# First batch on fp32 key chunks, values in column halves, a bound for A's scale

## The chip, the cores and the metric

The kernel runs on one core of one Trainium2 chip. The metric is the device time of one execution in microseconds (us), the median of several runs; a profile of one further execution shows where the time goes. Engines are named as in the profile: PE (TensorE), PEld (its weight loads), DVE (VectorE), ACT (ScalarE), POOL (GpSimd), SP (SyncE, which here only issues DMAs).

## The reference

Agent attention over 4 batches of 11456 tokens with 128 channels and 49 agents, then a mixture of 8 experts (128 to 1024 to 128) of which each token takes one:

```python
def _attn_ref(q, k, v, agents):
    a2k = sm(agents, k)          # softmax(scale * agents @ k^T): 49 x 11456 a batch
    agent_v = a2k @ v            # 49 x 128
    q2a = sm(q, agents)          # 11456 x 49
    return q2a @ agent_v
def _moe_ref(x, w_gate, w1, w2):
    expert_idx = np.argmax(x @ w_gate, axis=1)
    ...
    h = np.maximum(xe @ w1[e], 0.0)
    out[mask] = gate_w[mask, None] * (h @ w2[e])
```

## The kernel before

The 11456 tokens of a batch are 12 chunks: 11 of 128x8 tokens and a rest of 96x2. Per batch the kernel computes the key scores of all chunks and their maximum over the tokens, then exp and the sum of exp times values, which gives `av` (49 agents by 128 channels, twice side by side). From `av` it chooses the expert that most tokens are likely to take, loads that expert's w1 and w2 and forms A = av @ w1, so that for a query chunk the hidden layer is relu(E @ A), with E the exponentials of the query's scores, turned over by DMA (tile `M`). The loop over hidden layers, `experts`, has 184 steps a batch: `layer1` (L1204, L1205) multiplies 512 tokens by one 128-column piece of A in two fp16 parts `Ah`, `Al`; ACT and DVE make the two fp16 parts of its relu (`hh`, L1210, L1211); `layer2` (L1224) multiplies by w2. Tokens of other experts are left to gathered blocks at the end.

fp32 factors are split into two fp16 parts with a power-of-two scale. `prepare` does this for a chunk: `squares` (L332, ACT) gives the sum of squares, `scale_bits` (L212 to L219) the scale, then one of two forms. In form 'A', `split` (L360 on ACT, L362 on DVE) makes the parts `hl`, and `turn_over` (L387) transposes them by a DMA on SP's queue into `hT`. In form 'C' (keys of the first batch), `transposed` transposes the fp32 chunk on PE (L403), and ACT and DVE make the two parts from PSUM (L405, L406). `scores` then does three fp16 matmuls for each 128 tokens (L415 to L417). Values of the first batch are in form 'F': `values` multiplies fp32 exponentials by fp32 values (L522), whose output is 49 rows, and adds each chunk's result to `acc` (L533).

The first batch has nothing to run beside it: no hidden layer can start before its av, weights and A exist. Later batches do their attention in the shadow of the hidden layers of the batch before. Work is put on a list of events with due times in steps (`at`, `prepare`, the constants KS0 and so on), and the recording layer may then issue an instruction of an engine earlier if it is ready sooner. Chunks, w1 and w2 come into 11 buffers named `ld` (512 KB each) in turn; `load` asks for them `AHEAD` uses ahead. A load waits on SP's queue until the buffer of 11 tiles before is free. `weights` computes two column halves of A (`pa`, L734), their maximum (L741) and w2's (L743), a common scale (`pow2_scale`, over PE and DVE twice), and then Ah, Al (L755, L756) and w2's parts (L762, L763).

Of the kernel before, what the change touches and what calls it, by code (L numbers as in the profile page):

```python
# [22 lines left out]
A = 49  # L23
# [8 lines left out]
MODES = {'k': 'C', 'v': 'F', 'q': 'A'}  # L32
# [13 lines left out]
KS0, KT0, KL0, VT0, VL0, QS0, QT0, QL0 = -200, 2, 4, 2, 1, -146, 3, 5  # L46
# [20 lines left out]
AHEAD = 3  # L67
# [3 lines left out]
def agent_moe_kernel(ctx, tc, q, k, v, agents, wg, w1, w2, out):  # L71
# [33 lines left out]
    make_identity(nc, ident)  # L105
    ones = cpool.tile([P, P], F32, name="ones")
# [74 lines left out]
    def pow2_scale(amax, n):  # L181
# [9 lines left out]
        nc.tensor.matmul(pb[:, :n], ones[:n, :], dg[:n, :n], start=True, stop=True)  # L191
        pw = two.tile([P, 2], F32, tag="ppw", name="ppw")
# [11 lines left out]
    state = [dict() for _ in range(B)]  # L204

# [33 lines left out]
    def expert_weights(x, new, by_act=False):  # L239
# [6 lines left out]
        dma.dma_start(w2e, w2[ds(e, 1)].rearrange("e (p t) d -> (e p) (t d)", t=FT))  # L246
# [23 lines left out]
    def attention(b):  # L270
# [9 lines left out]
        def load(src, c):  # L280
            i = uses.index((b, src, c))
            for o in uses[:i + AHEAD]:
# [11 lines left out]
        def agent_squares():  # L294
            ag = AG["ag"] = one.tile([P, D], F32, tag="ag", name="ag")
            nc.sync.dma_start(ag[:A], agents[b])
# [14 lines left out]
        def agent_split():  # L311
            pt = small_ps()
            nc.tensor.transpose(pt[:, :A], AG["ag"][:A, :], ident[:A, :A])
            agh = AG["h"] = two.tile([P, A], F16, tag="agh", name="agh")
# [6 lines left out]
        def uniform(src, c):  # L321
            return src == "v" or how[src, c] == "C"

        def squares(src, c):
# [3 lines left out]
            x = load(src, c)  # L328
            jk = one.tile([P, CH], F16, tag="jk", name="jk")
# [6 lines left out]
        def total(src, c):  # L336
            p, ss = chunks[c][1], SC[src, c]
# [3 lines left out]
        def total2(src, c):  # L341
            if not uniform(src, c):
# [8 lines left out]
        def split(src, c):  # L351
            _, p, t = chunks[c]
# [41 lines left out]
        def transposed(src, c):  # L394
            _, p, t = chunks[c]
            x = load(src, c)
            xT = xpool.tile([P, 2, 8, P], F16, tag="hl", name="xT", bufs=HLB)
            m = SC[src, c][0][:, :1]
            for h in range(0, t, 4):
# [4 lines left out]
                pv = pt[:, :n * p].rearrange("d (i p) -> d i p", p=p)  # L404
                nc.scalar.activation(xT[:, 0, h:h + n, :p], pv, AF.Copy, scale=m)  # L405
# [17 lines left out]
        def kscores(c):  # L423
# [5 lines left out]
            pv, m = ps[:p, :t * A].rearrange("p (t a) -> p t a", a=A), SC["k", c][1][:p, :1]  # L429
            if first and c % 4 < SEV:  # L430
# [11 lines left out]
        def kmax(c):  # L442
# [7 lines left out]
            else:  # L450
                mx = MX["x"]
                nc.vector.tensor_tensor(mx[:p, :t, :], mx[:p, :t, :], sv, op=ALU.max)
# [32 lines left out]
        def kexp3(c):  # L485
            _, p, t = chunks[c]
            sc = S[c][:p, :t, :]
            if c == 0:
# [6 lines left out]
            if how["v", c] == "F":  # L495
                return
# [8 lines left out]

        def values(c):
            _, p, t = chunks[c]
            ps = either(first, psS, "s", psY, "y")
            if how["v", c] == "F":
                x, sc = load("v", c), S[c]  # L510
            else:
                (vh, vl), eh = TT.pop(("v", c)), EH.pop(c)
            for i in range(t):

                if how["v", c] == "F":
                    pairs = [(sc[:p, i, :], x[:p, i, :])]
                else:
# [855 lines left out]
```

## Time and profile before

| | us |
|---|---|
| median of 3 runs (1165.85 to 1166.94) | 1166.04 |
| the profiled execution: its own time | 1163.97 |
| its span, first to last instruction | 1162.2 |
| PE busy in the span | 1028.1 (88%) |
| DVE busy | 1016.7 (87%) |
| ACT busy | 840.4 (72%) |

The span is 1.8 us shorter than that execution's time, and that time is 2.07 us under the median. PE's granted clock is 0.961 of full speed over the span. Busy shares are averages: most of the span is the loop of hidden layers with PE and DVE both near 90%; the first 100 us, in which only the first batch's attention can run, look otherwise and are read stage by stage.

### The profile page before, as it was taken

How to read it: one execution, taken by the hardware profiler on the slowest of the kernel's cores; microseconds unless marked ns; L12 is line 12 of the kernel's file. 1: busy time of each engine (PE TensorE's matmuls, PEld its weight loads, DVE VectorE, ACT ScalarE, POOL GpSimd, SP SyncE). 2: the span in 40 equal slices, each digit the busy share in tenths (PEclk: the TensorE clock that was granted, in tenths of full speed). 3: DMA queues.
4: the chain of work that ended last, by engine and by line, in shares of the span. 5: the costliest groups of instructions: out<-in, count | busy, mean ns of one | idle time of the engine just before them, and what ended most of it. 6: DMA issues, size and time to landing. Idle time of an engine off the chain costs nothing. (4 is left out here: it accounts for less than half of the span.)

```text
span 1162.2 us, 36038 instructions
## 1 busy us (share of the span) xinstructions
PE 1028.1 (88%) x14607; PEld 827.9 (71%) x14607; DVE 1016.7 (87%) x2407; ACT 840.4 (72%) x1506; POOL 231.5 (20%) x369
## 2 busy tenths in 40 slices
PE   6757789988989989989988889999989988989895
PEld 5645668767867777777776677777767776767795
DVE  7867798889989988998989997999899988899794
ACT  8548786689669787798678885896585555756591
POOL 1301010035400110143300110245100213110133
PEclk9877999999998999999999999999999999999998
DMA  8489999371489899371499898450574544523370
GB/s 331 131 235 215 250 237 203 99 187 59 84 233 268 189 248 223 108 189 47 84 274 267 195 249 184 122 126 32 161 182 104 127 102 102 158 67 112 118 258 14
DMA packets 265673, 191.02 MB, mean 164 GB/s; under 512 B 217513, under 2 KB 230306, under 8 KB 265504
## 3 DMA queue, kind: packets, MB, share of 16 engines
q1 hardware_dynamic: 263648, 185.39, 62.9%
q0 software_dynamic: 1568, 2.25, 1.0%
q8 instruction: 115, 1.88, 0.7%
q10 hardware_dynamic: 288, 1.05, 0.3%
q14 instruction: 54, 0.44, 0.1%
HBM read 99.75 MB, written 36.43 MB: 117 GB/s over the span
## 5 line engine op out<-in xcount | busy, mean ns | idle before, releaser
L1224 PEld LDWEIGHTS <-hh 128*128 128x128 f16 x8640 | 555.4, 100 | 168.9 <-issue 9.8
L1224 PE MATMUL py<-w2h,hh 128*128 128x128 f16 (+1 forms) x5760 | 615.5, 222 | 4.2 <-issue 2.6
L1210 ACT ACTIVATE hh<-ph 128x512 f16<-128x512 f32 (+1 forms) x728 | 411.8, 586 | 183.0 <-PE ph L1205 164.4
L1224 PE MATMUL py<-w2l,hh 128*128 128x128 f16 (+1 forms) x2880 | 531.2, 222 | 0.0
L1211 DVE SCALAR_TENSOR_TENSOR hh<-ph,hh 128x512 f16<-128x512 f32 (+1 forms) x736 | 479.0, 667 | 47.1 <-ACT hh L1210 44.1
L1204 PE MATMUL ph<-M,Ah 128*128 128x512 f16 (+1 forms) x736 | 278.3, 378 | 26.1 <-DVE hh L1211 23.6
L1205 PE MATMUL ph<-M,Al 128*128 128x512 f16 (+1 forms) x736 | 279.0, 380 | 0.1
L362 DVE SCALAR_TENSOR_TENSOR hl<-ld,mul,hl 128x1024 f16<-128x1024 f32 (+1 forms) x120 | 147.7, 1234 | 13.6 <-ACT hl L360 13.1
L332 ACT ACTIVATE jk<-ld 128x1024 f16<-128x1024 f32 (+1 forms) x132 | 133.9, 1014 | 29.9 <-PE pa L734 10.4
L360 ACT ACTIVATE hl<-ld,mul 128x1024 f16<-128x1024 f32 (+1 forms) x120 | 130.7, 1095 | 21.2 <-DVE mul L216 20.4
L219 POOL TENSOR_SCALAR div<-hb,bits 128x1 int32<-128x1 int32 (+1 forms) x96 | 39.9, 425 | 363.5 <-DVE hb L212 312.8
L1205 PEld LDWEIGHTS <-Al 128*128 128x128 f16 x736 | 72.4, 98 | 33.5 <-issue 30.4
L1204 PEld LDWEIGHTS <-Ah 128*128 128x128 f16 x736 | 73.7, 100 | 6.3 <-issue 3.5
L415 PEld LDWEIGHTS <-hT 128*128 128x128 f16 (+1 forms) x630 | 53.2, 98 | 20.3 <-DMA hT<-hl 19.5
L415 PE MATMUL ps_s<-agh,hT 128*128 128x49 f16 x572 | 54.1, 187 | 14.8 <-DMA hT<-hl 11.0
L1237 DVE TENSOR_TENSOR yo<-py,cs 128x512 f32<-128x512 f32 (+1 forms) x92 | 61.3, 666 | 0.2 <-PE py L1224 0.2
L219 POOL TENSOR_SCALAR div<-hb 128x1 int32<-128x1 int32 (+3 forms) x45 | 14.0, 312 | 223.4 <-DVE hb L212 198.0
L416 PE MATMUL ps_s<-agl,hT 128*128 128x49 f16 x572 | 53.8, 186 | 0.0
L417 PE MATMUL ps_s<-agh,hT 128*128 128x49 f16 x572 | 53.7, 186 | 0.0
L416 PEld LDWEIGHTS <-hT 128*128 128x128 f16 (+1 forms) x630 | 52.1, 98 | 2.3 <-issue 1.7
L417 PEld LDWEIGHTS <-hT 128*128 128x128 f16 (+1 forms) x630 | 51.6, 98 | 0.3
L493 POOL TENSOR_TENSOR es<-es,S 128x392 f32<-128x392 f32 (+1 forms) x39 | 41.3, 1060 | 40.3 <-ACT S L483 31.7
(304 smaller groups left out, 1385.9 us busy)
## 6 DMA issues: line engine op xcount, KB each, us to landing
ld<-in_k_dram SPq DMA_DIRECT2D x44, 512.0 KB
ld<-in_v_dram SPq DMA_DIRECT2D x44, 512.0 KB
ld<-in_q_dram SPq DMA_DIRECT2D x44, 512.0 KB
out_dram<-yo SPq DMA_DIRECT2D x88, 256.0 KB
w1e<-in_moe_w_dram SPq DMA_DIRECT2D x17, 512.0 KB
w2e<-in_moe_w_dram SPq DMA_DIRECT2D x17, 512.0 KB
exps<-E SPq DMA_DIRECT2D x44, 196.0 KB
wn<-in_moe_w_dram SPq DMA_DIRECT2D x16, 512.0 KB
```

The costliest lines, as they stand in the source:

```text
L332: nc.scalar.activation(jk[:p, :t * D], x[:p, :t, :].rearrange("p t d -> p (t d)"), AF.Square, accum_out=ss[:p])
L360: nc.scalar.activation(hi[:p, :t, :], x[:p, :t, :], AF.Copy, scale=m)
L362: nc.vector.scalar_tensor_tensor(lo[:p, :t, :], x[:p, :t, :], m, hi[:p, :t, :], op0=ALU.mult, op1=ALU.subtract)
L415: nc.tensor.matmul(o, x[:, 0, i, :p], AG["h"], start=True, stop=False)
L416: nc.tensor.matmul(o, x[:, 0, i, :p], AG["l"], start=False, stop=False)
L417: nc.tensor.matmul(o, x[:, 1, i, :p], AG["h"], start=False, stop=True)
L1204: nc.tensor.matmul(ph[:, :nn], st['Ah'][:, f, :], m, start=True, stop=False)
L1205: nc.tensor.matmul(ph[:, :nn], st['Al'][:, f, :], m, start=False, stop=True)
L1210: nc.scalar.activation(hh[:, 0, :nn], ph[:, :nn], AF.Relu)
L1211: nc.vector.scalar_tensor_tensor(hh[:, 1, :nn], ph[:, :nn], 0.0, hh[:, 0, :nn], op0=ALU.max, op1=ALU.subtract)
L1224: mm_ = lambda l, r, **k: nc.tensor.matmul(o, l, r, skip_group_check=True, **k)
L1237: nc.vector.tensor_tensor(yo[:p, :n, :], py[:p, :n * D].rearrange("p (i d) -> p i d", d=D), cs.unsqueeze(2).broadcast_to([p, n, D]), op=AL ...
```

## The change

It rebuilds the first batch. Of its 12 key chunks four full ones and the rest are in a new form 'X', and its first query chunk too: no squares, no scale and no parts; the fp32 chunk is transposed on PE, copied from PSUM in two halves (one by ACT, one by DVE) and multiplied in fp32 (one matmul, no longer three) by the fp32 agents. The values' matmuls go in turn to two halves of PE's columns (output rows 0 to 48 and 64 to 112 of two PSUM tiles) and accumulate over all chunks; `both` adds the halves when the result is transposed. Of the subtractions of the maximum three go to POOL, and the sum of exponentials is kept in two accumulators, one on POOL, one on DVE. For all batches A's scale comes from a bound, max|w1| of a row times max|av|, summed over rows, and w2's from ACT's sum of squares, so neither needs A. The weights of the first batch are loaded by SP, no longer by ACT. `queued` puts the splits of the first two batches behind the choice of the expert on DVE ("D") and their DMA transposes behind w2's load on SP ("S"). `WO` sets the steps of `weights` in later batches.

```diff
-MODES = {'k': 'C', 'v': 'F', 'q': 'A'}
+MODES = {'k': 'XCCXCCXCCXCX', 'v': 'F', 'q': 'X'}
-KS0, KT0, KL0, VT0, VL0, QS0, QT0, QL0 = -200, 2, 4, 2, 1, -146, 3, 5
+KS0, KT0, KL0, VT0, VL0, QS0, QT0, QL0 = -200, 2, 4, 2, 1, -172, 3, 2.5
-AHEAD = 3
+AHEAD, AHEAD0 = 3, 8
+WO = (0, 2.5, 5, 9.5, 11, 12.5)
+KXP, ESP = (2, 5, 8), (0, 2, 4, 6, 8)
...
+    both = cpool.tile([P, A], F32, name="both")
+    nc.vector.tensor_tensor(both, ident[:, :A], ident[:, 64:64 + A], op=ALU.add)
...
+    def queued(x):
+        return tc.issue_after(gate[x].ins) if x in gate else nullcontext()
...
         def squares(src, c):
...
+            if how[src, c] == "X":
+                return
...
         def transposed(src, c):
...
+                if whole:
+                    if h:
+                        nc.vector.tensor_copy(xT[:, h:h + n, :p], pv)
+                    else:
+                        nc.scalar.copy(xT[:, h:h + n, :p], pv)
+                    continue
...
         def scores(src, c, ps):
...
+                if how[src, c] == "X":
+                    nc.tensor.matmul(o, x[:, i, :p], AG["T"], start=True, stop=True)
+                    continue
...
-            if first and c % 4 < SEV:
+            if first and c % 4 == 1:
                 nc.vector.tensor_scalar(sv, pv, m, None, op0=ALU.mult)
...
         def kexp(c):
...
-            nc.vector.tensor_tensor(sc, sc, MX["b"][:p].unsqueeze(1).broadcast_to([p, t, A]), op=ALU.subtract)
+            eng = nc.gpsimd if first and c in KXP else nc.vector
+            eng.tensor_tensor(sc, sc, MX["b"][:p].unsqueeze(1).broadcast_to([p, t, A]), op=ALU.subtract)
...
         def kexp3(c):
...
+            if first:
+                j = 0 if c in ESP else 1
+                if c < 2:
+                    AV["es", j] = one.tile([P, 8, A], F32, tag=("es", "mx")[j], name="es")
+                    (nc.gpsimd, nc.vector)[j].tensor_copy(AV["es", j], sc)
+                else:
+                    es = AV["es", j]
+                    (nc.gpsimd, nc.vector)[j].tensor_tensor(es[:p, :t, :], es[:p, :t, :], sc, op=ALU.add)
+                return
...
+        def values_wide(c):
...
+                AV["half"] = [psY.tile([P, 512], F32, tag="y", name="pv") for _ in range(2)]
+            for i in range(t):
+                r, ps = 64 * (i % 2), AV["half"][i % 2]
+                nc.tensor.matmul(ps[r:r + A, :D], sc[:p, i, :], x[:p, i, :], start=(c == 0 and i < 2),
+                                 stop=(c == NCK - 1 and i >= t - 2))
+            if c == NCK - 1:
+                acc = AV["acc"]
+                nc.vector.tensor_copy(acc[:A, :], AV["half"][0][:A, :D])
+                nc.vector.tensor_copy(acc[64:64 + A, :], AV["half"][1][64:64 + A, :D])
...
         def weights_load(ei):
-            AV["w1"], AV["w2"] = expert_weights(ei[0:1, 0:1], tiles(rest=(ldp, "ld")), first)
+            AV["w1"], AV["w2"] = expert_weights(ei[0:1, 0:1], tiles(rest=(ldp, "ld")))
...
             if i == 0:
...
+                nc.vector.tensor_reduce(am[:, 0:1], w1s, axis=AX.X, op=ALU.max, apply_absolute_value=True)
+                nc.vector.tensor_tensor(am[:, 1:2], am[:, 0:1], AV["avm"], op=ALU.mult)
...
+            elif i == 1:
...
+                nc.scalar.activation(jk[:, :FF], w2s, AF.Square, accum_out=s2)
+                pt = small_ps()
+                nc.tensor.matmul(pt[:, :1], ones, AV["am"][:, 1:2], start=True, stop=True)
+                AV["pw"], AV["inv"] = pow2_of(pt, 1)
```

Three places show what the edits move.

DVE between the subtraction of the keys' maximum (L478, now L528) and the sum `rs` (L544, now L613). Before, a piece of the second half (`acc` is the result of a values chunk, `hl` a split of a later chunk):

```order
L533 SCALAR_TENSOR_TENSOR acc<-ps_y,acc 49x128
L362 SCALAR_TENSOR_TENSOR hl<-ld,mul,hl 128x1024
L533 SCALAR_TENSOR_TENSOR acc<-ps_s,acc 49x128
...
L362 SCALAR_TENSOR_TENSOR hl<-ld,mul,hl 128x1024 x2
...
L544 TENSOR_SCALAR rs<-ps_small 128x49
```

Now, from the start of the stage (`mq`, `E`, `mm` belong to the first query chunk):

```order
L528 TENSOR_TENSOR S<-S,mxb 128x392 x2
L687 TENSOR_REDUCE mq<-ps_s 128x8
L528 TENSOR_TENSOR S<-S,mxb 128x392
L689 TENSOR_TENSOR E<-ps_s,mq 128x392
L542 COPY es<-S 128x392
...
L706 TENSOR_TENSOR mm_143<-E,mm_143 128x8x49
L528 TENSOR_TENSOR S<-S,mxb 128x392 x4
...
L606 TENSOR_REDUCE e_911<-es 128x49
L577 COPY acc<-pv 49x128
L578 COPY acc<-pv 49x128
L613 TENSOR_SCALAR rs<-ps_small 128x49
```

The splits have left this stage, the eleven additions to `acc` have become two copies, and the first query's four operations have come in.

SP's queue from the first query's loads on. Before:

```order
L387 DMA_TRANSPOSE hT<-hl 128x16x128 x3
L1300 DMA exps<-E 128x392
L573 DMA avd<-ava 49x128
L640 DMA_TRANSPOSE M<-mm_141 128x8x128
L287 DMA ld<-in_q_dram 128x1024
```

Now:

```order
L712 DMA_TRANSPOSE M<-mm_143 128x8x128
...
L302 DMA ld<-in_q_dram 128x1024 x2
L302 DMA ld<-in_k_dram 128x1024
...
L258 DMA w1e<-in_moe_w_dram 128x1024
...
L260 DMA w2e<-in_moe_w_dram 128x1024
...
L302 DMA ld<-in_q_dram 128x1024
L417 DMA_TRANSPOSE hT<-hl 128x16x128 x3
L302 DMA ld<-in_k_dram 128x1024
L417 DMA_TRANSPOSE hT<-hl 128x16x128 x2
```

The transposes of the splits stand behind w2's load, and seven loads stand ahead of w1's.

ACT from the weights on. Before:

```order
L755 ACTIVATE Ah<-pa,pinv 128x8x64 x2
L762 ACTIVATE w2h<-w2e,pinv 128x1024
L687 ACTIVATE Ld<-Ld 128x64
L332 ACTIVATE jk,ss<-ld 128x1024
L1210 ACTIVATE hh<-ph 128x512 x4
```

Now (L355 squares and L389 split later chunks):

```order
L824 ACTIVATE jk,s_992<-w2e 128x1024
L319 ACTIVATE jk,sa<-ag 49x128
L809 ACTIVATE Ah<-pa,pinv 128x8x64
L355 ACTIVATE jk,ss<-ld 128x1024
L809 ACTIVATE Ah<-pa,pinv 128x8x64
L849 ACTIVATE w2h<-w2e,mul 128x1024
...
L1297 ACTIVATE hh<-ph 128x512
...
L389 ACTIVATE hl<-ld,mul 128x1024 x3
```

The first split now follows the first hidden layer's `hh`; before, four splits had run ahead of it.

## Rows read from the trace of the kernel before

**Rows 1.** Stretches: engines' busy us (instructions), then clock, DMA share, GB/s.

```profile
0.00:43.10 43.10, 25.95 (x378) 22.95 (x378) 32.06 (x103) 30.32 (x56) 6.35 (x28) 0.89 0.75 273
43.10:66.60 23.50, 22.07 (x194) 21.57 (x194) 18.16 (x40) 13.65 (x23) 8.10 (x8) 0.90 0.45 109
66.60:78.90 12.30, 5.10 (x27) 2.71 (x25) 5.74 (x27) 0.71 (x1) 0.00 (x0) 0.70 0.99 238
78.90:104.50 25.60, 14.06 (x152) 7.59 (x152) 20.18 (x59) 22.40 (x37) 4.00 (x9) 0.63 0.93 262
104.50:200.00 95.50, 85.23 (x1251) 68.49 (x1249) 82.23 (x178) 73.25 (x129) 11.00 (x19) 0.94 1.09 234
200.00:1162.00 962.00, 875.67 (x12617) 704.58 (x12614) 858.31 (x2003) 700.09 (x1260) 202.09 (x305) 0.98 0.60 150
```

**Rows 2.** Timeline of SP's issues and of ACT: first key loads, first use.

```profile
1.67 6.90 SPq L287 DMA_DIRECT2D ld<-in_k_dram  x11
...
5.66 1.06 ACT L332 ACTIVATE jk<-ld 128x1024 f16<-128x1024 f32 x1 [2.09 <-DMA ld<-in_k_dram]
```

**Rows 3.** Groups of instructions, 0 to 43.1 us: busy, mean ns, idle before.

```profile
L406 DVE SCALAR_TENSOR_TENSOR xT<-pxT,mul,xT 128x512 f16<-128x512 f32 x22 | 15.2, 744 | 1.6 <-ACT xT L405 1.6
L405 ACT ACTIVATE xT<-pxT,mul 128x512 f16<-128x512 f32 x22 | 13.6, 693 | 2.8 <-DVE hb L212 2.8
L332 ACT ACTIVATE jk<-ld 128x1024 f16<-128x1024 f32 x11 | 11.7, 1061 | 2.6 <-DMA ld<-in_k_dram 2.3
...
L433 ACT ACTIVATE S<-ps_y,div 128x392 f32<-128x392 f32 x3 | 1.8, 595 | 1.3 <-PE ps_y L417 1.3
```

**Rows 4.** Timeline of PE: fp32 weight loads of transposes, one fp32 matmul of 49 columns.

```profile
20.38 0.75 PEld L403 LDWEIGHTS pxT<-ident,ld 128*128 128x128 f32 x7
...
65.92 0.42 PE L542 MATMUL ps_small<-e,ones 128*128 128x49 f32 x2
```

**Rows 5.** Timeline of the values' stage: DVE, PE with its loads, POOL.

```profile
43.13 3.61 DVE L478 TENSOR_TENSOR S<-S,mxb 128x392 f32<-128x392 f32 x5
...
51.55 1.50 DVE L478 TENSOR_TENSOR S<-S,mxb 128x392 f32<-128x392 f32 x3
...
49.48 1.91 PE L522 MATMUL ps_y<-ld,S 128*49 128x128 f32 x16
...
49.37 1.76 PEld L522 LDWEIGHTS ps_y<-ld,S 128*49 128x49 f32 x16
...
49.32 1.21 POOL L493 TENSOR_TENSOR es<-es,S 128x392 f32<-128x392 f32 x1 [0.74 <-DVE es L493]
```

**Rows 6.** Line 522: duration of its loads, ns min/median/max.

```profile
L522 PEld LDWEIGHTS ps_y<-ld,S x96: 124/124/203, 44.4 to 65.0; 128*49 128x49 f32 x96
```

**Rows 7.** Timeline: expert chosen (DVE), weights issued (ACT), w2 first read (DVE).

```profile
70.54 0.13 DVE L713 CAST ei<-ep 128x1 int32<-128x1 f32 x1
...
71.69 0.40 ACTq L244 DMA_DIRECT2D w1e<-in_moe_w_dram  x1
...
78.90 1.22 DVE L743 TENSOR_REDUCE am<-w2e 128x1 f32<-128x1024 f32 x1 [0.16 <-DMA w2e<-in_moe_w_dram]
```

**Rows 8.** Stretches as in rows 1: a DMA transpose alone; weights and loads alone.

```profile
62.00:64.00 2.00, 2.00 (x20) 2.00 (x19) 1.59 (x2) 1.42 (x2) 0.00 (x0) 1.00 1.16 213
74.00:86.00 12.00, 6.28 (x19) 2.85 (x20) 6.03 (x27) 6.07 (x10) 0.98 (x3) 0.50 1.03 391
```

**Rows 9.** Timeline of PE and SP before the first `layer2`.

```profile
96.42 3.46 SPq L387 DMA_TRANSPOSE hT<-hl  x1
...
103.54 0.22 PE L415 MATMUL ps_y<-agh,hT 128*128 128x49 f16 x1 [2.98 <-DMA hT<-hl]
...
104.55 0.28 PE L1224 MATMUL py<-w2h,hh 128*128 128x128 f16 x1
```

**Rows 10.** A later batch, 560 to 660 us: PE's waits; the reductions of A.

```profile
PE ps_small L191 <- DVE hb L212: 2.3, 1, 2.3
...
L741 DVE TENSOR_REDUCE am<-a x2: 677/682/686, 590.9 to 595.7; 128x1 f32<-128x512 f32 x2
```

More of the change, by code (lines that the diff above doesn't have):

```diff
@@ L281, in load @@
             i = uses.index((b, src, c))
-            for o in uses[:i + AHEAD]:
+            for o in uses[:i + (AHEAD0 if first else AHEAD)]:
                 if o not in loaded:
@@ L294, in agent_squares @@
         def agent_squares():
-            ag = AG["ag"] = one.tile([P, D], F32, tag="ag", name="ag")
-            nc.sync.dma_start(ag[:A], agents[b])
+            for x in range(b, min(b + 2, B)):
+                if x not in agents_in:
+                    agents_in[x] = two.tile([P, D], F32, tag="ag", name="ag")
+                    nc.sync.dma_start(agents_in[x][:A], agents[x])
+            ag = AG["ag"] = agents_in[b]
             nc.vector.tensor_scalar(ag[:A], ag[:A], scale, None, op0=ALU.mult)
@@ L351, in split, with split1 @@
         def split(src, c):
+            with queued("D") if b < 2 else nullcontext():
+                split1(src, c)
+        def split1(src, c):
             _, p, t = chunks[c]
@@ L504, in kexp3 @@
             EH[c] = eh
+        def values_wide(c):
+            _, p, t = chunks[c]
+            x, sc = load("v", c), S[c]
+            if c == 0:
+                AV["acc"] = one.tile([P, D], F32, tag="acc", name="acc")
+                nc.gpsimd.memset(AV["acc"], 0.0)
+                AV["half"] = [psY.tile([P, 512], F32, tag="y", name="pv") for _ in range(2)]
+            for i in range(t):
+                r, ps = 64 * (i % 2), AV["half"][i % 2]
[5 more added lines that the diff above has]
+                nc.vector.tensor_copy(acc[64:64 + A, :], AV["half"][1][64:64 + A, :D])
@@ L527, in values @@
+            o = ps[:, :A]
+            div = SC["v", c][1][:P, :1]
             if c == 0:
-                AV["acc"] = one.tile([P, D], F32, tag="acc", name="acc")[:A] if first else one.tile([P, D], F32, tag="acc", name="acc")[:, :A]
+                AV["acc"] = one.tile([P, D], F32, tag="acc", name="acc")[:, :A]
             acc = AV["acc"]
@@ L552, in agentvalues @@
                     pt = small_ps()
-                    nc.tensor.transpose(pt[:, :A], AV["acc"], ident[:A, :A])
+                    nc.tensor.matmul(pt[:, :A], AV["acc"], both, start=True, stop=True)
                     AV["acc"] = pt[:, :A]
@@ L609, in qscores @@
             _, p, t = chunks[c]
[L610 removed]
+            ps = either(first and how["q", c] != "X", psS, "s", psY, "y")
             scores("q", c, ps)
@@ L724, in weights, with product, halves @@
             H = FF // 2
+            def product(j):
+                pa = AV["a2", j] = psH.tile([P, 512], F32, tag="h", name="pa") if first else small_ps()
+                nc.tensor.matmul(pa[:, :H], AV["av"], w1s[:, j * H:(j + 1) * H], start=True, stop=True)
+            def halves(j):
+                m = AV["inv"][:, 0:1]
+                x = AV["a2", j][:, :H].rearrange("a (p t) -> a t p", t=FT)
+                o = slice(j * P // 2, (j + 1) * P // 2)
+                nc.scalar.activation(st["Ah"][:, :, o], x, AF.Copy, scale=m)
+                nc.vector.scalar_tensor_tensor(st["Al"][:, :, o], x, m, st["Ah"][:, :, o],
+                                               op0=ALU.mult, op1=ALU.subtract)
@@ L786, in attention @@
         tk = ks + kt * (NCK - 1) + kl + 2
-        for i in range(3):
+        for i in range(1 if first else 0, 3):
             at(base + tk + i, keymax, i)
@@ L810, in attention @@
         for i in range(6):
-            at(base + tw + w0 + i * w1_, weights, i)
+            at(base + tw + w0 + (i * w1_ if first else WO[i]), weights, i)
         tw += w0 + 5 * w1_
```

139 lines of the change are left out of this document (74 added, 65 removed).

## The prediction

> **What bounds the kernel now.** I read the busy time by stretches first [rows 1]. From 200 us on PE is busy 875.7 of 962 us and DVE 858.3: the loop of hidden layers, which the change hardly touches. The room is ahead of it. The first `layer2` starts at 104.55 us [rows 9], and until then PE worked 67 of 104.5 us, much of it on what a shadow would hide. So I took the stages one by one from the timelines and asked which wait ends last in each.
>
> Keys, to 43.1 us: eleven loads of 512 KB are issued from 1.67 us and the first is in use at 5.66 [rows 2], so a load takes 4.0 us alone. From there ACT is the fullest engine for the work that it has, 30.3 us, with DVE at 32.1 of which some is set-up, and PE at 26.0 [rows 1]. Values, 43.1 to 66.6: PE is busy 22.1 of 23.5 us. A chunk is 16 passes (8 matmuls, two passes each for fp32), and the weight loads of one chunk take 1.76 us [rows 5], 0.110 a pass, without gaps. Weights, 66.6 to 78.9: a chain of small steps until the expert is known at 70.54 (+0.13), w1's issue at 71.69 and w2's first use at 78.90 [rows 7]; DMA moves 238 GB/s here and is busy, since other loads go beside it. Start-up, 78.9 to 104.5: A's scale, Ah and Al, the first hidden layers, and then PE waits for DMA transposes of later chunks: its last wait, 2.98 us, ends at 103.54, for the second query split [rows 9].
>
> **The change part by part**, against the profiled execution, 1163.97 us; the median is 2.07 higher.
>
> Keys. Four full chunks and the rest lose their squares (4 x 1.06 us on ACT), eight fp16 parts on ACT (8 x 0.69) and eight on DVE (8 x 0.74) [rows 3]. They gain one copy of 128x512 from PSUM on ACT and one on DVE; the first query gains the same. No copy of this kind is in the trace; ACT's neighbours are 0.595 (392 columns) and 0.693 (512, scaled) [rows 3], so 5.5 copies at 0.65 are 3.6 us. Three more evictions of scores go from DVE to ACT, 3 x 0.6 = 1.8. ACT: -4.2 - 5.5 + 3.6 + 1.8 = -4.3. DVE gives up 8 x 0.74 + 1.8 and takes 5.5 copies of at most 0.74: -3.6. PE takes fp32 scores: a chunk is 8 matmuls of two passes, whose price lies between a weight load of 128 columns (0.75/7 = 0.107) and half of the one such pair, which includes its latency (0.42/2 = 0.21) [rows 4]: 1.7 to 3.4 us a chunk, 7 to 14 for 4.25 chunks, and 0.9 for the query's transposes. PE's 26.0 then becomes 34 to 41, before the fp16 matmuls that go. So ACT's 4.3 us can be had if passes cost near the lower price, which I take since they stand in a stream; X chunks also wait for no scale (ACT's 2.8 us for `hb` [rows 3]). I take **4**, bounds -3 (PE bound) and 7.
>
> Values. The stage now has two candidates. PE: the first query's scores stand ahead of the values (16 passes, 1.7 us), then 180 passes for 11.25 chunks. If the halves do not run side by side they cost 180 x 0.110 = 19.8 us as now; if fully, 9.9. The trace has no matmuls side by side. [...] DVE: 8 subtractions, 4 operations of the first query, one copy, 5 additions and 2 reductions, about 20 of 128x392. Without POOL beside them such an operation is 0.50 apart (1.50/3), with POOL 0.72 (3.61/5) [rows 5]. POOL has 3 subtractions, a copy and 4 additions, some 9 us at 1.21 [rows 5]; in these DVE does 12.5 operations, the other 7.5 take 3.8, and 0.7 leads to `rs`: 13.5 us. I take the halves as overlapping, because each has its own columns and its own PSUM tile and alternates with the other, so that PE (1.1 + 1.7 + 9.9 = 12.7) is just under DVE. 23.5 becomes 13.5: **10**, bounds 0.3 and 11.5 (all of DVE at 0.50).
>
> Weights. The first query's operations have left the chain to the choice, one comparison goes and one maximum comes: 0.5. w1 and w2 have SP's queue to themselves if the seven loads ahead of them are through. Those wait for buffers of values chunks and for `M`'s transpose; at 391 GB/s [rows 8] a load is 1.34 us, seven 9.4, and they can begin about 6 us into the values' stage, so they end near 15.5, and w1 is issued at about 13.5 + 3.5 + 1.1 = 18. Then w2 is in use 4.0 + 1.3 = 5.3 us after w1's issue, where it took 7.2 [rows 7]. 0.5 + 1.9 = **2.4**, bounds -1 (loads not through) and 4.
>
> Start-up. From w2's landing ACT must do its square sum, the agents' squares, Ah, a chunk's squares, Ah, w2h, another's squares, hh, again squares and an exponential, about 9.4 us, and then the first split, 1.1; DVE adds 1.3: 11 us. SP's queue has a load ahead of the transposes that needs the second split's buffer: 12. Two loads (2.7) go first, then five transposes, each 0.52 MB at 213 GB/s [rows 8], 2.5 us, with one more load between: 12 + 2.5 + 12.3 + 1.3 = 28, and 1 for the scores. So `layer2` starts 29 us after w2's landing where it was 104.5 - 78.9 = 25.6: the splits that ran under the weights' wait are late now. **-3.4**, bounds -10 and 3.
>
> From the first `layer2` on, the order of every engine is the old one but for single rows. The old cover of the moved splits is gone, and that is the -3.4; nothing else is late then, since the loads of those chunks are early.
>
> Later batches. Each loses two DVE reductions of 0.68 [rows 10] (w1's maximum takes w2's place) and one of PE's waits inside `pow2_scale`, 2.3 us [rows 10]; ACT's two copies make room for the square sum. DVE is 89% busy, so 3 x 1.36 = 4.1 is worth **3**, bounds 0 and 7. The wider steps of `weights` move its operations by at most two steps, which I cost at nothing: DVE and ACT beside them are the cover.
>
> Sum: 4 + 10 + 2.4 - 3.4 + 3 = 16.0. 1163.97 - 16.0 = 1148.0 profiled, 2.07 more for the median: **1150**.
>
> **The rivals.** (1) The halves do not overlap. The values' stage is 1.1 + 1.7 + 19.8 + 0.6 = 23.2, its gain 0.3 and the sum 6.3: 1160. For it: no row shows overlap. Against: the halves share no columns. (2) DMA binds the start-up. Share 0.93 to 1.09 from 78.9 to 200 us [rows 1] and SP's transposes that then take 3.46 to issue [rows 9] speak for it: two transposes that ran under the weights' wait come back at that price, 6.9, besides the 3.4. The sum is 16.0 - 6.9 = 9.1: 1157. Against: the seven loads are earlier. (3) PE binds the keys through the fp32 passes at 0.21: 16.0 - 7 = 9: 1157. (4) On the other side: a half's weight load does not run under the other half's matmul. Then a pass costs load and stream, 0.124 [rows 6] + 0.110 = 0.234, 180 of them 42.1 us, the stage 45.5 instead of 23.5, and the sum 16.0 - 10 - 22 = -16: 1182. It decides from 0.145 us a pass (stage 29.5) on. Against: loads and matmuls of the same columns overlap now, or a chunk would not take 1.76 for 16 passes [rows 5]. [...] (5) No change: the first batch's gain is eaten at the start of the loop, within 2.3 us of 1166.
>
> **How the numbers follow.** Forecast 0.52, its own range 1144 to 1155; (1) 0.17, (2) 0.15, (3) 0.06, (5) 0.04, (4) 0.06. 0.2% is 2.3 us, about what a measurement of this kernel tells from no change. Faster: 0.52 + 0.17 + 0.15 + 0.06 = 0.90, same 0.04, slower 0.06. The range reaches down to all terms near their good ends (7 + 11.5 + 4 + 0 + 3.5 = 26: 1140) and up past (1): 1140 to 1161.
>
> **What would show it.** Right: mxb copied near 39 us, `rs` near 52.5, w2 read near 62.5, first `layer2` near 91.5; PE's values about 1 us a chunk, in pairs that start together. Wrong: values at 1.75 us a chunk (1), or at over 2.3 (4); PE waiting for `hT` past 95 us (2); gaps of ACT and DVE in the keys with PE full (3). The forecast falls if the stages gain as written and the distance from first `layer2` to the end grows by more than 5 us.

## The result, and the profile after

The changed kernel takes **1157.2 us** (median of 8 runs, 1154.23 to 1162.67); the kernel before, timed beside it, 1167.95 (1165.85 to 1170.86). The ratio is 0.9905, 95% interval 0.9878 to 0.9932: faster by 1%. The forecast was 1150 with a range of 1140 to 1161, so sign and range held, and the middle was 7 us too low.

Four later groups of runs timed the kernel before again, at medians of 1173 to 1174 us; the changed kernel was repeated in one of them and stood at 1156.83, ratio 0.9838 (0.9807 to 0.9868). The two intervals don't touch, because the kernel before moved by 6 us between groups and the changed one did not. Why is not known. The gain is thus 10.7 to 17 us in medians, and below I compare two pairs of profiled executions: the first (1163.97 us before, 1159.84 after) and a repeat of each (1171.69 and 1160.68).

The stretches of the first changed execution, cut where the stages end. Columns as in [rows 1].

```profile
0.00:42.90 42.90, 31.83 (x349) 29.23 (x349) 27.36 (x89) 24.90 (x46) 4.82 (x24) 1.00 0.79 286
42.90:59.20 16.30, 15.60 (x200) 15.02 (x199) 14.53 (x26) 7.08 (x13) 8.64 (x8) 0.80 0.55 175
59.20:68.60 9.40, 3.37 (x12) 2.02 (x12) 5.05 (x23) 0.00 (x0) 0.00 (x0) 0.70 0.81 304
68.60:96.90 28.30, 17.30 (x156) 9.58 (x156) 21.16 (x65) 24.55 (x41) 3.40 (x10) 0.56 0.84 185
96.90:200.00 103.10, 90.86 (x1356) 72.43 (x1354) 86.73 (x184) 79.78 (x142) 9.68 (x19) 0.95 1.01 222
200.00:1158.00 958.00, 871.17 (x12517) 698.46 (x12513) 849.18 (x1989) 691.48 (x1254) 197.44 (x308) 0.98 0.61 151
```

Against [rows 1]: the keys' stage is as long as it was (42.9 for 43.1), though ACT has 24.9 us of work there instead of 30.3; the values' stage fell from 23.5 to 16.3; the weights' from 12.3 to 9.4; the start-up grew from 25.6 to 28.3. By the marks of both pairs, in us (stages end at the copy of `mxb`, the keys' maximum; at `rs`, the sum of exponentials; at w2's first read; at the first `layer2`):

| | forecast | first pair | repeats |
|---|---|---|---|
| keys | 4 | 42.89 to 42.72: 0.2 | 43.08 to 42.24: 0.8 |
| values | 10 | 23.67 to 16.42: 7.3 | 23.68 to 16.40: 7.3 |
| weights and start-up | 2.4 - 3.4 = -1.0 | 37.99 to 37.74: 0.3 | 38.67 to 37.53: 1.1 |
| sum at the first `layer2` | 13.0 | 7.7 | 9.3 |
| from there to the end | 3 | 1057.65 to 1061.1: -3.5 | 1064.6 to 1062.7: 1.8 |

Weights and start-up stand as one, since the repeat of before first reads w2 behind another reduction; in the first pair they are 2.9 and -2.6. PE in the first batch (its timeline: eight transposes and the scores of the first X chunk, the scores of the second, those of the first query, the values, the first `layer2`, the first wait in the loop):

```profile
5.55 1.97 PE L437 MATMUL pxT<-ident,ld 128*128 128x128 f32 x8 [0.64 <-DMA ld<-in_k_dram]
...
10.95 3.65 PE L456 MATMUL ps_y<-agT,xF 128*128 128x49 f32 x16 [0.92 <-ACT xF L443]
...
20.87 1.88 PE L456 MATMUL ps_s<-agT,xF 128*128 128x49 f32 x16
...
42.61 3.65 PE L456 MATMUL ps_s<-agT,xF 128*128 128x49 f32 x16
46.19 11.53 PE L573 MATMUL pv<-ld,S 128*49 128x128 f32 x180
...
96.88 0.28 PE L1311 MATMUL py<-w2h,hh 128*128 128x128 f16 x1
...
103.02 0.36 PE L721 MATMUL ps_s<-Gs,M 128*128 128x18 f16 x8 [2.46 <-DMA M<-mm]
```

The same 16 passes of scores take 3.65 us at 10.95 and 1.88 at 20.87, a factor of 1.94. At 42.61, after PE had waited for DVE, the passes cost 3.65 again, and there (44 to 46 us) the clock column of the profile shows 0.50, where it shows 1.00 from 20 to 22 us: the factor is that of TensorE's granted clock. Over the first stretch it shows 1.00 throughout, at 10.95 too; there I read the clock from the durations. All 180 passes of values take 11.53 us, where the old 180 filled the 23.5 us stage.

### The profile page after: what moved, and what is told of

Its sections match the earlier page's. It is cut to its first block, busy times and chain, and to the rows that moved or that the text cites. A ratio compares the mean times of both kernels' runs of the same rounds, so it can differ in the third digit from the quotient of the medians.

```text
span 1158.0 us, 35852 instructions
## 1 busy us (share of the span) xinstructions
PE 1030.1 (89%) x14575; PEld 826.7 (71%) x14575; DVE 1004.0 (87%) x2372; ACT 827.8 (71%) x1495; POOL 224.0 (19%) x369
## 3 DMA queue, kind: packets, MB, share of 16 engines
q8 instruction: 115, 1.88, 0.7%
## 5 line engine op out<-in xcount | busy, mean ns | idle before, releaser
L389 ACT ACTIVATE hl<-ld,mul 128x1024 f16<-128x1024 f32 (+1 forms) x119 | 129.8, 1100 | 22.1 <-DVE mul L230 21.8
L355 ACT ACTIVATE jk<-ld 128x1024 f16<-128x1024 f32 (+1 forms) x126 | 129.0, 1024 | 18.1 <-DMA ld<-in_q_dram 6.9
L233 POOL TENSOR_SCALAR div<-hb,bits 128x1 int32<-128x1 int32 (+1 forms) x90 | 31.2, 358 | 351.5 <-DVE hb L226 293.3
L1292 PEld LDWEIGHTS <-Al 128*128 128x128 f16 x736 | 72.8, 99 | 28.3 <-issue 26.8
L721 PE MATMUL ps_s<-Gs,M 128*128 128x18 f16 x318 | 14.8, 172 | 33.0 <-DMA M<-mm 31.9
```

The lines of the kernel that those rows point to most:

```text
L355: nc.scalar.activation(jk[:p, :t * D], x[:p, :t, :].rearrange("p t d -> p (t d)"), AF.Square, accum_out=ss[:p])
L389: nc.scalar.activation(hi[:p, :t, :], x[:p, :t, :], AF.Copy, scale=m)
L1292: nc.tensor.matmul(ph[:, :nn], st['Al'][:, f, :], m, start=False, stop=True)
```

## The experiments

Ratios are to the kernel before, timed in the same group of runs.

### The kernels again

`after_again` is the changed kernel, `before_again` the kernel before; no edit.

> The changed kernel once more, unedited, for a second profile and as the yardstick of the other runs. Theory A (the gain that is missing against the forecast lies ahead of the first layer2): the stages repeat within 0.5 us (maximum of the keys in use at 42.9, sum of exponentials rs at 59.1, w2 read at 68.6, first layer2 at 96.9), and the loop behind it is 2 to 4 us shorter than in the kernel before. Rival B (the missing gain is given back in the loop): PE's wait of 3.8 us for a transposed M near 440 us is there again and the distance from first layer2 to the end is again some 3 us longer than in the kernel before. Time about 1157.

> The kernel before, unedited, for a second profile of its loop. In the first profile its loop took 1003.1 us from the first layer2 to the last scaled output, in the changed kernel's two profiles 1005.4 and 1006.5: by these nothing is gained in the later batches. Theory A (the later batches gain the forecast 3 us, and the first profile of the kernel before was a short one): about 1008 to 1010 here. Rival B (the later batches gain nothing): 1003 to 1006 again. The marks ahead of it repeat within 0.5 us: maximum in use at 43, rs at 66.6, first layer2 at 104.5.

After again: 1156.83 us, 0.9838 (0.9807 to 0.9868). Before again: 1171.57, 0.9974 (0.9941 to 1.0007), which holds 1: no difference from itself, as it should be. The marks of the table follow from their profiles. What repeats within 0.1 us is the values' gain, 7.3. What doesn't repeat is the time after the first `layer2`: 1057.65 and 1064.6 in two executions of one kernel. The first profile of before, on which the prediction rests, was a short one.

Within one kernel the time goes with the granted clock of the run: over all recorded runs, a run whose mean clock is 0.001 lower than its kernel's other runs of that group is about 0.7 us longer (an estimate by a straight line through the 128 runs whose clock is on record). So where the clock differs I give it beside the medians below.

### Do the halves run side by side?

```diff
-                r, ps = 64 * (i % 2), AV["half"][i % 2]
+                r, ps = 0, AV["half"][i % 2]
...
-                nc.vector.tensor_copy(acc[64:64 + A, :], AV["half"][1][64:64 + A, :D])
+                nc.vector.tensor_copy(acc[64:64 + A, :], AV["half"][1][:A, :D])
```

All values' passes go to the same columns, in turn to the two tiles.

> The values' matmuls go to one half of PE's columns, the rest is unchanged. If the two halves run side by side (a pass went from 0.100 to 0.048 us at the full clock in the profiles), the stage is bound by PE again: some 14 passes at 0.2 us, 166 at 0.1, so the values end near 65.5 and rs is at 67 instead of 59.1: 7 to 8 us longer, about 1165. If the stage is bound by DVE in either case, the time grows by less than 2 us.

1165.8 us, 0.9922 (0.9892 to 0.9952), 9 us slower than the changed kernel in the same group. Its PE timeline, and two stretches inside its values' stage:

```profile
45.09 21.57 PE L573 MATMUL pv<-ld,S 128*49 128x128 f32 x180
```

```profile
58.00:62.00 4.00, 4.00 (x39) 4.00 (x37) 0.00 (x0) 0.00 (x0) 0.00 (x0) 1.00 0.94 322
...
50.00:66.00 16.00, 16.00 (x149) 16.00 (x148) 7.55 (x13) 2.65 (x5) 2.29 (x3) 1.00 0.78 251
```

Stretches of the changed kernel's values' stage, in the same columns:

```profile
46.00:48.00 2.00, 2.00 (x20) 1.88 (x21) 1.70 (x4) 1.14 (x4) 1.92 (x3) 0.50 0.00 0
50.00:52.00 2.00, 2.00 (x42) 2.00 (x40) 2.00 (x4) 0.14 (x2) 1.03 (x1) 1.00 0.55 174
...
50.00:56.00 6.00, 6.00 (x114) 6.00 (x112) 6.00 (x9) 2.67 (x6) 3.29 (x3) 1.00 0.81 208
```

A stretch counts every pass that it touches, so short ones count a few too many (the 0.048 us of the expectation comes from that); the difference of two stretches is free of it. At full clock one half alone does 149 - 39 = 110 passes in 12 us, 0.109 each; two halves do 114 - 42 = 72 in 4 us, 0.056 each, and by the starts of single passes in the trace a pair takes 0.109 us, 0.055 a pass. That is twice as fast, and at a granted clock of 0.50 two halves (20 passes touched in 2 us) about match one half at 1.00 (39 in 4). So rivals (1) and (4) fall. For (4) the loads would have to stand apart from the matmuls, but a pass each 0.055 us has no room for a load of 0.124 us (the median of the changed kernel's 180, as in [rows 6]) that overlaps no running matmul. How they overlap, no run here tells.

One half's stage lasts 25.5 us (41.74 to 67.27) where the changed kernel's lasts 16.4: the halves are worth 9.1 us in the stage and 9 in the median, about half of the 17 us that the changed kernel gains in this group. In `one_half` DVE, ACT and POOL stand at 0.00 from 58 to 62: PE alone binds. In the changed kernel something else does.

### What binds the values' stage now

DVE's timeline in the changed kernel, then POOL's:

```profile
42.72 0.21 DVE L518 COPY mxb<-ps_small 128x49 f32<-128x49 f32 x1 [0.61 <-PE ps_small L516]
42.97 1.80 DVE L528 TENSOR_TENSOR S<-S,mxb 128x392 f32<-128x392 f32 x2
46.30 0.57 DVE L687 TENSOR_REDUCE mq<-ps_s 128x8 f32<-128x392 f32 x1 [1.54 <-PE ps_s L456]
...
48.85 0.55 DVE L545 TENSOR_TENSOR es<-es,S 128x392 f32<-128x392 f32 x1
...
50.08 1.38 DVE L706 TENSOR_TENSOR mm<-E,mm 128x392 f16<-128x392 f32 x1
...
54.11 1.38 DVE L545 TENSOR_TENSOR es<-es,S 128x392 f32<-128x392 f32 x1
...
59.14 0.21 DVE L613 TENSOR_SCALAR rs<-ps_small 128x49 f32<-128x49 f32 x1
```

```profile
49.73 1.30 POOL L545 TENSOR_TENSOR es<-es,S 128x392 f32<-128x392 f32 x1 [1.49 <-ACT S L533]
52.73 2.35 POOL L545 TENSOR_TENSOR es<-es,S 128x392 f32<-128x392 f32 x2 [1.70 <-ACT S L533]
```

DVE's only wait is 1.54 us for the first query's scores; otherwise it works from 42.7 to 59.1. Two of its operations on two tiles take 1.38 us, where one that has no POOL beside it (48.85) takes 0.55. Both started while POOL was at work on a sum, and end 0.43 and 0.41 us after POOL's (51.03, 55.08): as if they had waited for it; what would hold them there, the traces don't show. `no_pool` gives POOL's share to DVE:

```diff
-KXP, ESP = (2, 5, 8), (0, 2, 4, 6, 8)
+KXP, ESP = (), (0, 2, 4, 6, 8)
...
-                (nc.gpsimd, nc.vector)[j].tensor_tensor(...)
+                nc.vector.tensor_tensor(...)
```

(and the copy likewise)

> The changed kernel, but in the values' stage POOL has nothing to do: its three subtractions and five additions or copies go to DVE. In the changed kernel DVE operations of 128x392 that lie beside POOL's take 0.90 to 1.38 us, those without 0.48 to 0.55 apart. If DVE is slowed by POOL as much as POOL takes off it, the stage (maximum in use to rs) stays at 16.4 plus or minus 1 us: DVE has 28 operations of 0.5 us, two reductions of 0.8 and the wait for the query's scores. If POOL's help is real, the stage grows by 8 x 0.5 = 4 us to 20.

1164.42 us, 0.9924 (0.9897 to 0.995). DVE in its profile:

```profile
38.76 0.21 DVE L518 COPY mxb<-ps_small 128x49 f32<-128x49 f32 x1 [0.82 <-PE ps_small L516]
39.01 1.04 DVE L528 TENSOR_TENSOR S<-S,mxb 128x392 f32<-128x392 f32 x2
42.34 0.56 DVE L687 TENSOR_REDUCE mq<-ps_s 128x8 f32<-128x392 f32 x1 [2.29 <-PE ps_s L456]
...
45.09 0.56 DVE L706 TENSOR_TENSOR mm<-E,mm 128x392 f16<-128x392 f32 x1
...
55.97 0.21 DVE L613 TENSOR_SCALAR rs<-ps_small 128x49 f32<-128x49 f32 x1
```

The two subtractions fall from 1.80 to 1.04 and L706 from 1.38 to 0.56. The stage lasts 17.2 us with a wait of 2.29 in it, so 14.9 without; the changed kernel's 16.4 less 1.54 is 14.9 too. What POOL takes over, DVE loses by the longer operations beside it. The median is 7 us worse than the changed kernel's in other groups (1157), and the intervals of the ratios don't touch. By the estimate above some 5 us of that go with the granted clock, 0.954 in the mean of these nine runs and 0.961 in those of `after_again` (among the nine alone the time does not follow the clock); why it was lower, and the rest, is open.

`k0_q` moves the first query's scores ahead of the maximum, on top of the next section's `k0_copies_dve`:

```diff
-KS0, KT0, KL0, VT0, VL0, QS0, QT0, QL0 = -200, 2, 4, 2, 1, -172, 3, 2.5
+KS0, KT0, KL0, VT0, VL0, QS0, QT0, QL0 = -200, 2, 4, 2, 1, -172.5, 3, 3
```

(and the query's matmuls have an event of their own at step -171.2)

> Both copies of the first key chunk on DVE, and the first query's scores issued ahead of the maximum's two PE steps, where PE stood still and its clock was still full. In the changed kernel these 16 passes took 3.65 us at the low clock behind the maximum, and DVE waited 1.54 us for them. Expected: the passes take 1.9 us; the query's four DVE operations fall into the maximum's waits, which makes the maximum some 1 us later than 38.3; the sum rs then comes about 14 us after the maximum instead of 16.4, near 53.5 (54.75 without the move). If DVE alone binds the stage, rs does not move by more than 0.5 us.

1156.87 us, 0.9854 (0.981 to 0.99): no gain. The stage is 15.8 us, but `mxb` comes at 42.10 where `k0_copies_dve` alone has 38.30. Some 2 of these 3.8 us go with the clock, which rose later here (15.4 us against 10.0; `k0_ks1`, with 15.4 too and no move, has 40.37). The rest is about what the query's four DVE operations take (2.0 us): their price had only moved ahead.

### The keys: X chunks and the clock

Three kernels try the forms and the first copies. `keys_all_C` makes all keys 'C' again, `first_chunk_C` moves the four full X chunks one place on, so that a C chunk is first, and `k0_copies_dve` takes the first chunk's copies away from ACT, whose squares PE had waited behind (0.92 us at 10.95 above):

```diff
-MODES = {'k': 'XCCXCCXCCXCX', 'v': 'F', 'q': 'X'}
+MODES = {'k': 'C', 'v': 'F', 'q': 'X'}
```

```diff
-MODES = {'k': 'XCCXCCXCCXCX', 'v': 'F', 'q': 'X'}
+MODES = {'k': 'CXCCXCCXCCXX', 'v': 'F', 'q': 'X'}
```

```diff
-                    if h:
+                    if h or (src == "k" and c == 0):
```

> All key chunks in form C (two scaled parts, three fp16 matmuls), as in the kernel before; first query and all else as changed. Theory A: the fp32 chunks bring nothing in the keys' stage, since PE took what ACT and DVE gave up: the maximum of the keys in use at 42 to 44 instead of 42.9, time within 1.5 us of the changed kernel. If the fp32 chunks are worth the forecast 4 us, it is at 47 and the time 1161.

> As many key chunks in fp32 as in the changed kernel, but chunks 1, 4, 7, 10 and the rest instead of 0, 3, 6, 9 and the rest: PE begins with the transposes of two chunks and fp16 scores, as in the kernel before, and the first fp32 scores come third. Theory A (PE holds the low clock longer when fp32 scores are among its first work; until 17 to 18.7 us in four profiles of the changed order, until 10.0, 15.4 and 15.4 us with the first chunk's copies on DVE, until about 10 us in the kernel before): the full clock is there by 11 us and the maximum in use by 38 to 39.5 instead of 41.7 to 42.9, first layer2 3 us earlier. Rival: the clock rises when it does whatever the work, the maximum stays at 41.5 to 43.

> Both copies of the first key chunk from PSUM on DVE; in the changed kernel ACT's copy stood behind the squares of a later chunk and PE waited 0.92 us for it. [...] If the clock does not depend on that gap, only the 0.9 us of the wait can be had, and less where the later loads bind: at most 1 us.

- `keys_all_C`: 1161.76 us, 0.9862 (0.9823 to 0.9901), and `mxb` at 45.63. Against 42.72 in the changed kernel the X chunks are worth about 3 us. The value isn't clean: the 96 transposes that both kernels have took PE 19.9 us there and 17.8 in the changed kernel (346 and 326 ns each).
- `first_chunk_C`: 1160.3 us, 0.9893 (0.9845 to 0.994), `mxb` at 43.48. A miss: its clock, read from the durations, is full from about 12.4 us on (the second chunk's 16 fp32 passes take 1.88 at 13.03) and still the stage is no shorter. Near its end DVE waits 1.83 us for a C chunk's scores (36.66) and 1.11 us for the query's transposes (38.99), both ahead of the last maximum; that is 2.9 of the some 5 us that are missing, and the rest is open. With another order it doesn't compare with the others, but an early clock alone is not enough.
- `k0_copies_dve`: 1156.1 us, 0.9839 (0.9802 to 0.9877): in the median equal to the changed kernel (1156.83 in that group). But its profiled execution is the shortest of all, 1154.46, with `mxb` at 38.30.

This looked as if the 0.92 us gap held PE's clock low. It falls by two other executions. The PE timeline of `after_again`, the unchanged order:

```profile
10.27 3.65 PE L456 MATMUL ps_y<-agT,xF 128*128 128x49 f32 x16
```

No gap, and the clock is low as before (the second chunk's passes take 1.89 at 20.19). And of `no_pool`, which has the changed kernel's order over the whole keys' stage:

```profile
5.54 1.97 PE L437 MATMUL pxT<-ident,ld 128*128 128x128 f32 x8 [0.98 <-DMA ld<-in_k_dram]
...
9.85 1.99 PE L456 MATMUL ps_y<-agT,xF 128*128 128x49 f32 x16
...
11.70 1.07 PE L437 MATMUL pxT<-ident,ld 128*128 128x128 f32 x8
```

Here the first scores take 1.99 instead of 3.65 and the transposes behind them 1.07 instead of 1.97. The full clock is there at about 9.9 us, and `mxb` comes at 38.76. Over the executions that start with an X chunk and have no further work in this stage, `mxb` follows the clock (read from the durations of the passes): full at 9.9 to 10.0 us, 38.76 and 38.30; at 15.4, 40.37 (`k0_ks1`, below); at 17 to 18.7, 42.72, 42.24, 42.29 and 41.74. The same order gives 38.76 and 42.72, so the keys' term is 0.2 to 4.1, by when the clock rises. Two kernels tried to raise it. `warm` has 28 small matmuls of constants before the first load lands:

```diff
+    def warm(n):
+        pt = psH.tile([P, 512], F32, tag="h", name="warm")
+        for _ in range(n):
+            nc.tensor.matmul(pt[:, :P], ones16, ones16, start=True, stop=True)
+
+    warm(28)
```

> The changed kernel with 28 added bf16 matmuls of constants (128x128) on PE while it waits for the first key load; their result is not read. In five profiles of the changed order of instructions the full clock came at 17 to 18.7 us four times (maximum in use at 41.7 to 42.7) and at 9.9 us once (38.8). Theory A (the forecast's 4 us of the keys are there whenever the clock is full early, and are lost when it is not): the full clock is there by 10 us, the maximum in use at 37 to 39 and the first layer2 at 92 to 94. Rival B (the early maximum had another cause): 41.7 to 42.7 as in the other profiles. The median falls by up to 4 us against 1157 if the loop leaves the gain.

1162.16 us, 0.9895 (0.9852 to 0.9937), `mxb` at 43.85: a miss. Stretches of its profile:

```profile
8.00:10.00 2.00, 1.74 (x9) 1.70 (x9) 0.16 (x1) 1.37 (x5) 0.29 (x1) 0.50 1.04 416
...
16.00:18.00 2.00, 2.00 (x24) 1.94 (x22) 1.58 (x3) 1.75 (x4) 0.00 (x0) 0.51 1.03 422
18.00:20.00 2.00, 2.00 (x39) 1.97 (x38) 1.52 (x5) 1.90 (x4) 0.28 (x1) 1.00 1.04 396
```

The first eight transposes took 1.09 us, so the clock was up. Then PE stood still from 6.9 to 8.3 us, and from there the granted clock is 0.50 until 18 us, over work that leaves PE few gaps. `warm_all` adds `k0_copies_dve` and two groups of fillers, fp32 matmuls with no reader, in PE's waits before `mxb`: five (ten passes, 3.56 us) behind the last scores and six (twelve passes, 1.44 us) behind the maximum's transposition:

> As the run before, with the first chunk's copies on DVE, and more matmuls that nobody reads behind the last key scores (fp32, on finished scores) and behind the maximum's first transposition, so that PE does not stand still for 2.5 us ahead of the first query's scores and the values. If the low clock is what makes the query's 16 passes take 3.65 us and DVE wait for them 1.5 us: the passes take 1.9, the wait is gone, the values' stage (maximum in use to rs) falls from 16.4 to about 14.5; maximum near 37.5, rs near 52, first layer2 near 90. If the clock falls all the same, the stage stays at 16.4.

1159.06 us, 0.9872 (0.9837 to 0.9908). With the same 28 matmuls ahead its first eight transposes took 1.97 us, so by the durations the clock was low from there on, until about 19.9 us. The fillers delayed the matmuls to `mxb`, 44.64. But they did keep the clock for the first query:

```profile
44.53 1.99 PE L462 MATMUL ps_s<-agT,xF 128*128 128x49 f32 x16
47.48 11.59 PE L588 MATMUL pv<-ld,S 128*49 128x128 f32 x180 [0.97 <-ACT S L548]
```

The scores took 1.99 instead of 3.65, DVE did not wait, and still the stage lasted 16.2 us. DVE's operations beside POOL became longer instead:

```profile
48.88 0.87 DVE L543 TENSOR_TENSOR S<-S,mxb 128x392 f32<-128x392 f32 x1
...
50.97 1.18 DVE L717 CAST mm<-E 128x392 f16<-128x392 f32 x1
```

The first takes 0.55 and the second 0.35 in the changed kernel, where POOL did more of its work while DVE waited. So DVE with POOL beside it is the bound, at 16.2 to 16.4 with the wait or without. A kernel with neither POOL's share nor the wait was not run; by `no_pool` its stage would last about 14.9 us (an estimate).

### The start-up

SP's and ACT's timelines in the changed kernel:

```profile
78.86 8.31 SPq L417 DMA_TRANSPOSE hT<-hl  x3
```

```profile
68.62 1.06 ACT L824 ACTIVATE jk<-w2e 128x1024 f16<-128x1024 f32 x1 [12.54 <-DMA w2e<-in_moe_w_dram]
```

The first transposes of the splits start at 78.86, 15 us behind w2's issue at 63.90; ACT waits 12.54 us for w2 and only then turns to squares and splits. `k0_ks1` puts two splits under the weights' wait (on top of `k0_copies_dve`):

```diff
-KS1 = []
+KS1 = [-141.5, -140.2]
```

> Both copies of the first key chunk on DVE, and the first two key chunks of batch 1 are given earlier steps, so that their squares and splits stand on ACT and DVE under the wait for w1 and w2 and their transposes right behind w2's load on SP. Theory of the start-up (w2 read to first layer2 took 28.3 us in the changed kernel because ACT and DVE make the first split only after w2 is there, then five transposes follow one another): the first transposes are issued 1 to 3 us after w2's issue instead of 15, two of five are through when the others come, and the distance from w2's read to the first layer2 falls from 28 to 20 to 23 us; first layer2 near 87 instead of 93.2, the time 5 us less. Rival: the DMA engines are full there anyway (w1, w2 and loads), so the distance stays above 26 us.

1157.28 us, 0.9844 (0.9797 to 0.9892): no better in the median. SP's timeline shows that the edit did what it says:

```profile
65.50 0.34 SPq L260 DMA_DIRECT2D w2e<-in_moe_w_dram  x1
66.84 5.83 SPq L417 DMA_TRANSPOSE hT<-hl  x2
...
81.51 6.86 SPq L417 DMA_TRANSPOSE hT<-hl  x3
```

Two transposes now run 1.3 us behind w2's issue, and from w2's first read to `layer2` it takes 21.0 us instead of 28.3. But the splits' work on ACT and DVE lies in the values' stage, which ends 3.2 us later against `mxb`, and the first `layer2`, 91.46 against 93.17 in `k0_copies_dve`, is only 1.7 us earlier. Counted from `mxb`, which the clock put 2.1 us later here, the edit brings `layer2` forward by 3.8 us. From the first to the last scaled output it takes 1000.3 us, where the ten other executions with the new scale take 988.8 to 997.2: 3 to 11 us more, so the 3.8 are lost again in this execution. One profile doesn't show why the loop is longer.

### Later batches: the scale of A

```diff
+            if not first:
+                weights_later(i)
+                return
...
-            at(base + tw + w0 + (i * w1_ if first else WO[i]), weights, i)
+            at(base + tw + w0 + i * w1_, weights, i)
```

(`weights_later` is the old `weights`: scale from A and w2 by reductions)

> The changed kernel, but batches 1 to 3 take A's scale from the products again (two reductions of 0.68 us, a scale over PE and DVE twice, two copies by ACT) with the old steps. First batch unchanged, first layer2 at 96 to 97. If the bound for A's scale and the wider steps are worth the forecast 3 us in three batches, the loop (first layer2 to last scaled output) is 3 us longer than in the changed kernel's profiles (1005.4, 1006.5), the three switches of batch by about 1 us each; if they are hidden, it is within 1 us, which is what a median of this size can hardly tell, so the profile's marks at the switches decide.

1163.91 us, 0.9879 (0.9818 to 0.9941), 7 us above the two kernels of that group that have the new scale (1156.87, 1157.28); the intervals overlap, and the mean granted clock was lower, 0.961 against 0.964 and 0.966, which by the estimate above goes with 2 to 3.5 of the 7 us. The test that its expectation set, from the first `layer2` to the last scaled output, gives 1013.4 us, where the eleven other changed executions take 1002.1 to 1012.6, ten of them at most 1009.2. That is 4 to 11 us longer than those ten; but one kernel's own spread is nearly as large, 1003.1 and 1010.2 in the two executions of before. A gain by the new scale is likely, and its size is open. PE's waits from the first to the last scaled output, as totals, counts and means. The old kernel (`before_again`), then `later_old_scale`, then the changed kernel:

```profile
PE ps_s L649 <- DMA M<-mm: 14.2, 10, 2.9
...
PE ps_small L191 <- DVE hb L212: 4.7, 2, 2.3
PE ps_y L649 <- DMA M<-mm: 3.8, 2, 3.3
PE ps_small L191 <- DVE pdg L189: 2.9, 2, 2.7
```

```profile
PE ps_s L721 <- DMA M<-mm: 23.2, 11, 3.5
...
PE ps_small L195 <- DVE hb L226: 4.7, 2, 2.3
...
PE ps_small L195 <- DVE pdg L193: 3.1, 3, 2.7
```

```profile
PE ps_s L721 <- DMA M<-mm: 29.5, 14, 3.8
...
PE ps_y L721 <- DMA M<-mm: 5.4, 2, 5.0
```

The waits for the scale, 4.7 + 2.9 = 7.6 us, are gone with the bound (0.4 are left) and are back, 7.8, with the old scale. In their place PE waits for transposed `M`: 14.2 + 3.8 = 18.0 before (22.2 in the first profile of before), 29.5 + 5.4 = 34.9 after, and 30 to 42 in the other changed executions with the new scale. With the old scale it is 23.2 + 3.9 = 27.1: part of the growth goes with the scale, and part has another cause, which was not looked for. Those transposes stand on SP's queue among those for `hT`; that the latter became longer is not shown, since the longer pairs of them take 5.7 to 8.6 us in the two executions of before and 6.0 to 7.9 in the changed one.

## Why the prediction was right or wrong

- **Values** (10, measured 7.3). Right: the halves overlap in full (0.055 us a pass for 0.109), and DVE becomes the bound. Wrong is the step "in these DVE does 12.5 operations" at 0.72: beside POOL two take 0.90 each and two 1.38, where one alone takes 0.50 to 0.56. DVE's work is 14.9 us instead of 13.5, and 1.54 of waiting comes on top. That wait comes from another step that failed, PE's "1.7" for the first query's scores, which cost 3.65 at the low clock; but without it the stage was no shorter (16.2 in `warm_all`), so DVE beside POOL is what the 2.7 us went to.
- **Keys** (4, measured 0.2 and 0.8; 4.1 in `no_pool`). "if passes cost near the lower price" held for the later chunks, 0.1175 a pass, and failed for the first, 0.228. Rival (3) named that price but for all chunks and by latency; by the durations the low clock was the cause, and it costs more than those 16 passes, since all of PE is slow until 17 us or later (eight transposes take 1.95 us at 14.47 and 1.07 at 22.62). With the early clock of `no_pool` the term came out as forecast.
- **Weights** (2.4, measured 2.9): right; w1 was issued at 63.31, 4.2 us after `rs`, and w2 read 5.3 us later, as worked out.
- **Start-up** (-3.4, measured -2.6): right. The predicted distance was 29, measured 28.3. Rival (2) did not come in this stage: five transposes took 8.31 and 5.20 us, 2.6 to 2.8 each where 2.5 was forecast.
- **The start of the loop**, taken as the old order: from the first `layer2` to the first scaled output 14.3 us instead of 12.2. PE waits 2.46 us for `M` at 103.02. The next thing that was late stood there, and the prediction says "nothing else is late then".
- **Later batches** (3, bounds 0 and 7). Mechanism right: the waits for the scale go. The profiles say -3.5 and 1.8 for all that follows the first `layer2`, the medians with `later_old_scale` 7, of which 2 to 3.5 go with the clock. What of it stays is open; the saved wait turned partly into waits for `M`, for which the sum has no term. Of the -3.5, 1.1 lie behind the last scaled output, 55.7 us instead of 54.6. That repeats: 55.4 to 56.2 in all twelve changed executions, 54.4 and 54.6 in the two of before. Why was not settled.
- **The median** of the kernel before: I took 1166.04, and it was 1167.95 and 1174 in later groups. Against the latter the gain is 17 us, nearly my 16, but as a difference of other terms, so the sum was not right by that.

The forecast's own test, growth by more than 5 us after the first `layer2`, did not come true (3.5). By the first pair the profiled execution missed its forecast, 1148.0, by 11.8 us: 3.8 of keys, 2.7 of values and 6.5 after `layer2`, less 1.3 of weights and start-up. The median missed by 7 alone, since it lies 2.6 under the profiled execution and I had put it 2.1 above; that part is luck: 2.07 above its profiled execution the median would have been 1161.9, outside the range. The marks named as signs of being right came later than written: `mxb` 42.7 for 39, `rs` 59.1 for 52.5, w2 68.6 for 62.5, `layer2` 96.9 for 91.5. What holds is the halves, the weights and the start-up; the keys and the loop were not right in the pair that the forecast speaks of. Rival (5), no change, is out by the interval.

## What to carry to other kernels

Where matmuls have few output rows, 49 here, try sending them in turn to the two halves of PE's columns: it was worth 9.1 us here, about half of the gain. Then ask at once what is second: here DVE ended 1 to 2 us behind PE, and giving eight of its operations to POOL freed none of its time (14.9 us of work either way). Ask too what the next queue gives when an engine is freed in a loop: PE lost 7.6 us of waits for a scale here, and its waits for DMA transposes grew by more.

## What the runs showed of the hardware

- One order of instructions had TensorE's full clock, read from the durations of the passes, from 9.9 us in one execution and from 17 us or later in four executions of kernels with the same beginning, worth about 4 us at `mxb` (38.76 against 41.74 to 42.72). What decides it is open; the gap of 0.92 us did not, and 28 small matmuls ahead did not help (full clock from 18 and 19.9 us).
- The two halves of columns overlap in fp32 with loads and all: 0.055 us a pass at full clock against 0.109 in one half.
- Two DVE operations of 128x392 on two tiles that started beside POOL's took 1.38 us and ended 0.4 us after POOL's did; alone such an operation takes 0.50 to 0.56.
